# Fifteen small loads into the second K buffer, issued by ScalarE early in a decode block

## Chip, core and metric

The kernel runs on one core of one Trainium2 chip. A core has TensorE (PE), VectorE (DVE), ScalarE (ACT), GpSimd (POOL) and SyncE (SP), and 16 DMA engines that move data between the chip's memory (HBM) and the core's buffers. The metric is device time in microseconds (us); lower is better. The kernel before took 1309.94 us (median of 3 runs, 1309.94 to 1310.12).

## What is computed

One token for each of two sequences: a layer norm of x, a cached attention of 32 query heads over 8 key/value heads with 32768 cached positions, and a gated feed-forward branch that scales the attention's result. All data is float32.

```python
B, Sq, D = 2, 1, 512
Hq, Hkv, Sk, Dh = 32, 8, 32768, 128
...
q = (x @ wq).reshape(B, Sq, Hq, Dh).transpose(0, 2, 1, 3)
k = repeat(k_cache, Hq // Hkv, axis=1); v = repeat(v_cache, Hq // Hkv, axis=1)
p = softmax(einsum("bhqd,bhkd->bhqk", q, k) * Dh ** -0.5)
s = einsum("bhqk,bhkd->bhqd", p, v).transpose(0, 2, 1, 3).reshape(B, Sq, Hq * Dh) @ wo
...
gate = xn @ W_gate
h = gate * (gate > 0) * (xn @ W_up)
g = silu(h @ W_down)
...
xn = layernorm(x)
out = x + s * g
```

The two caches are 268 MB each; everything else is 28 MB. Every cached number is used once.

## The kernel before

The cache is read in 32 pieces of K and 32 of V (`PAIRS`), each of 8.39 MB: 128 partitions with one contiguous run of 64 KB each (`rows_of`, L413). Two K buffers, `kbuf[0]` and `kbuf[1]`, take the K pieces in turn (`load_kk`, L409); one more buffer of the same size, `wide`, takes first the query weights `wq`, then the gate and up weights together (`load_gu`, L544), then the down weights (`load_d`, L602), then one V piece after another (`load_vv`, L428). The output weights `wo` go into `kbuf[1]` at the end.

For each piece of K, VectorE transposes it in place (L660, eight instructions), TensorE forms the scores, and two steps later TensorE multiplies the weights with the V piece of the same positions. After every two pieces a softmax over one head group is finished.

All instructions are written out in one program order by a small class, `Program`. Each operation names the tiles it reads and writes; `op` (L39) derives the semaphore waits. An engine executes its own operations strictly in that order, so a wait also holds up what follows on the same engine. Every DMA goes through `load` (L239): it is issued by SyncE unless `engine="ACT"` is given, and it counts 16 on the semaphore named as its third argument when it has landed.

Before the main loop the order is as follows. SyncE issues `wq` into `wide` (L261) and the first K piece (`load_kk(0)`, L877), which wait for nothing. ScalarE issues two loads of x, of 2 rows of 2 KB (`xp`, in `st0`) and of 8 rows of 512 B (`xy`), at L289 and L290. VectorE computes the layer norm's statistics from `xp`; ScalarE takes the square root (L373 to L377); VectorE's reciprocal (L378) and normalization follow, and TensorE transposes the result. `project_q` (L456) multiplies it by `wq`. When that has freed `wide`, SyncE issues gate and up (`load_gu`) and, right behind them, the second K piece (`load_kk(1)`, L880), whose buffer is empty and which waits for nothing of its own. Inside the loop SyncE then issues the down weights and the third K piece at step 0, and from then on a V piece and a K piece at every step, each when its buffer has been read.

The rows named DMA queue in the profile are q1, which carries SyncE's loads, q10, which carries ScalarE's, and q8 and q14, which carry the engines' instruction code.

Of the kernel before, what the change touches and what calls it, by code (L numbers as in the profile page):

```python
# [162 lines left out]
def decode_block_kernel(nc, x, kc, vc, wq, wo, wg, wu, wd, out):  # L163
# [17 lines left out]
    def sbuf(name, *shape, align=32):  # L181
        return nc.alloc_sbuf_tensor(name, list(shape), F32, align_bytes=align)[:]
# [4 lines left out]
    kbuf = [sbuf(f"k{i}", P, 2 * NC * NR * DH, align=ALIGN) for i in range(2)]  # L187
# [42 lines left out]
    def dve(fn, r=(), w=()):  # L230
        pg.op("DVE", fn, r, w)
# [7 lines left out]
    def load(dst, src, sem, r=(), w=(), engine="SP"):  # L239
        pg.op(engine, lambda e: e.dma_start(dst, src), r, w, dma=sem)  # L240
# [12 lines left out]
    def group(g):  # L253
        return g % B, g // B
# [42 lines left out]
    for kb in range(4):  # L297
        dve(
            lambda e, kb=kb: e.memset(block_of[Q * kb : Q * kb + Q, kb * REP : (kb + 1) * REP], 1.0),
            w=["block_of"],  # L300
# [27 lines left out]
    n = 1  # L328
    while n < Q:
# [45 lines left out]
        ["stat", "eps"],  # L375
        ["stat"],
    )  # L377
    dve(lambda e: e.reciprocal(stat[:, 4:5], stat[:, 3:4]), ["stat"], ["stat"])  # L378
    dve(
        lambda e: e.tensor_scalar(xc, xc, stat[:, 4:5], None, op0=ALU.mult),  # L380
# [10 lines left out]
                lambda e, k=k: e.transpose(  # L391
                    px[:, k * 32 : (k + 1) * 32], xquad[:, k, :], ident[:32, :32]
                )
# [12 lines left out]
    def k_keys(b):  # L406
        return [f"k{b}"] + [f"k{b}_{i}_{c}" for i in range(2) for c in range(NC)]

    def load_kk(j):  # L409
        b = j % 2  # L410
        load(kbuf[b], rows_of(kc, 2 * j), f"k{b}", w=k_keys(b))

    def rows_of(src, t):  # L413
        b, hk = group(t // NU)
        lo = (t % NU) // 2 * 2 * TK
        return src[b, hk, lo : lo + 2 * TK, :].rearrange("(p r) d -> p (r d)", p=P)
# [431 lines left out]
    def project_far():  # L848
# [26 lines left out]
        )  # L875

    load_kk(0)  # L877
    project_q()
    load_gu()
    load_kk(1)  # L880

    for j in range(PAIRS + 2):
# [47 lines left out]
        if j + 2 < PAIRS:  # L930
            load_kk(j + 2)
# [64 lines left out]
```

## Time and profile before

| | |
|---|---|
| time, median of 3 | 1309.94 us |
| span of the profiled execution | 1308.4 us |
| time and span apart | 1.5 us |
| PE busy | 859.0 us (66%) |
| DVE busy | 718.1 us (55%) |
| ACT busy | 51.4 us (4%) |
| DMA, mean over the span | 432 GB/s |
| loads of K, issue to landing | 48.2 us (median of 32) |
| loads of V, issue to landing | 29.6 us (median of 31) |

The profile shows one execution. Its span runs from the first to the last recorded instruction of the core; the time measured from outside is 1.5 us longer. A DMA "packet" in it is one contiguous piece that one of the 16 DMA engines moves, or the count that an engine posts on a semaphore when its part of a load is done (these are the packets under 512 B). A load that is issued while others are still under way queues behind them, so the time from issue to landing is mostly queueing where it is much longer than the bytes need.

### The profile page before, as it was taken

To read this page: it belongs to the slowest core of one execution; us is meant where nothing else is said; L and a number is where in the kernel's file an instruction comes from. 1 tells how busy PE (TensorE), PEld (TensorE's weight loads), DVE (VectorE), ACT (ScalarE), POOL (GpSimd) and SP (SyncE) were. 2 spreads that over 40 slices of the span, in tenths; PEclk is the share of its full clock that TensorE was granted. 3 is DMA by queue.
4 is the path that set the end of the run, shared out by engine and by line. 5 is a ranking of instruction groups with operands and counts; after the bars stand their busy time and mean duration, and the time that the engine had idled before them with its cause. 6 is when DMAs were issued, how large, how long until landed. Compare 5 with 4: busy or idle time off the path is not lost.

```text
span 1308.4 us, 11146 instructions
## 1 busy us (share of the span) xinstructions
PE 859.0 (66%) x4720; PEld 211.5 (16%) x4720; DVE 718.1 (55%) x690; ACT 51.4 (4%) x133; POOL 10.5 (1%) x38
## 2 busy tenths in 40 slices
PE   3566675785666587576667667667665757865676
PEld 1111111211111121111111112121111112111121
DVE  3566654565655456664546666455665545656521
ACT  0001000000000000000000000000000000000000
POOL 0000000000000000000000000000000000000000
PEclk9677788878878887878898778798887889788788
DMA  9999999999999999999999999999999999999998
GB/s 417 423 438 435 437 431 441 425 439 429 437 429 439 435 433 441 429 441 427 439 429 437 429 439 435 433 441 429 441 427 439 429 437 429 439 435 433 439 431 357
DMA packets 10693, 564.79 MB, mean 432 GB/s; under 512 B 1195, under 2 KB 1211, under 8 KB 1597
## 3 DMA queue, kind: packets, MB, share of 16 engines
q1 hardware_dynamic: 10668, 564.67, 99.7%
q8 instruction: 6, 0.10, 0.0%
q14 instruction: 3, 0.02, 0.0%
q10 hardware_dynamic: 16, 0.01, 0.0%
HBM read 564.67 MB, written 0.00 MB: 432 GB/s over the span
## 4 chain that ended last, share of the span: by engine, by line
DMA 64%; DVE 17%; PE 15%; issue 4%; SPq 0%
DMA k<-in_A_k_cache_dram 58%; DVE k L660 17%; PE o L243 8%; PE s L243 6%; DMA k<-in_A_wo_dram 3%; DMA w<-in_A_wq_dram 2%; PE m_ps L243 1%; PE m_ps L693 0%; PE d L243 0%; SPq L240 0%; DVE gy L870 0%; DVE gy L872 0%
## 5 line engine op out<-in xcount | busy, mean ns | idle before, releaser
L243 PE MATMUL s<-k,qcur 128*32 128x512 f32 x2048 | 504.5, 710 | 370.5 <-DVE k L660 370.3
L660 DVE STREAM_TRANSPOSE k<-k 128x2048 f32<-128x2048 f32 x256 | 565.2, 2275 | 147.0 <-DMA k<-in_A_k_cache_dram 147.0
L243 PE MATMUL o<-w,wt 128*16 128x512 f32 x1984 | 245.5, 596 | 9.0 <-DMA w<-in_A_v_cache_dram 9.0
L243 PEld LDWEIGHTS s<-k,qcur 128*32 128x32 f32 x2048 | 89.5, 123 | 785.0 <-DVE k L660 639.3
L737 DVE STREAM_TRANSPOSE wt<-pt 128x512 f32<-128x512 f32 x64 | 45.9, 717 | 139.4 <-PE pt L243 134.6
L678 DVE TENSOR_SCALAR_CACHE_REDUCE st<-s 128x512 f32<-128x512 f32 x64 | 43.0, 672 | 120.9 <-PE s L243 120.9
L243 PEld LDWEIGHTS o<-w,wt 128*16 128x16 f32 x1984 | 62.4, 98 | 167.5 <-issue 167.5
L722 ACT ACTIVATE st<-st,nb 128x512 f32<-128x512 f32 x64 | 45.4, 710 | 1111.0 <-DVE nb L719 1111.0
L243 PE MATMUL pt<-st,perm 128*128 128x512 f32 x128 | 72.6, 696 | 1.5 <-ACT st L722 1.5
L763 DVE RECIPROCAL rl<-m_ps 128x1 f32<-128x1 f32 x16 | 2.7, 169 | 111.0 <-PE m_ps L243 111.0
L243 PE MATMUL m_ps<-ob,heads 128*128 128x128 f32 x128 | 21.7, 321 | 29.0 <-DVE ob L777 29.0
L243 PEld LDWEIGHTS pt<-st,perm 128*128 128x128 f32 x128 | 25.3, 219 | 34.4 <-issue 30.1
L803 DVE STREAM_TRANSPOSE os<-m_ps 128x512 f32<-128x512 f32 x16 | 11.5, 717 | 23.2 <-PE m_ps L243 23.2
L243 PEld LDWEIGHTS m_ps<-ob,heads 128*128 128x128 f32 x128 | 18.0, 217 | 31.1 <-DVE ob L777 31.1
L243 PE MATMUL m_ps<-w,wt 128*32 128x512 f32 (+1 forms) x128 | 16.2, 640 | 8.1 <-DMA w<-in_A_wq_dram 8.1
L777 DVE SCALAR_TENSOR_TENSOR ob<-o,share,ob 128x128 f32<-128x128 f32 x48 | 16.9, 351 | 1.7
L530 POOL TENSOR_TENSOR qcur<-qall,block_of 128x128 f32<-128x128 f32 x16 | 6.5, 406 | 1008.3 <-PE s L243 974.0
L243 PE MATMUL m_ps<-negone,mrow 1*128 1x1 f32 x32 | 6.0, 256 | 9.3 <-DVE mrow L708 9.3
L722 ACT ACTIVATION_READ_ACCUMULATOR st<-st,nb 128x1 f32 x64 | 11.9, 186 | 0.0
L481 DVE COPY os<-m_ps 128x512 f32<-128x512 f32 x2 | 1.4, 692 | 16.3 <-PE m_ps L243 16.3
L243 PE MATMUL o<-k,wt 128*16 128x512 f32 x64 | 8.4, 687 | 2.8 <-DMA k<-in_A_v_cache_dram 2.8
L391 PE MATMUL m_ps<-ident,st 32*128 32x32 f32 x4 | 0.7, 307 | 14.0 <-DVE st L380 14.0
(80 smaller groups left out, 102.8 us busy)
## 6 DMA issues: line engine op xcount, KB each, us to landing
k<-in_A_wo_dram SPq DMA_DIRECT2D x1, 4096.0 KB, 37.3
w<-in_B_W_gate_dram SPq DMA_DIRECT2D x1, 3584.0 KB, 19.6
w<-in_B_W_up_dram SPq DMA_DIRECT2D x1, 3584.0 KB, 27.6
w<-in_B_W_down_dram SPq DMA_DIRECT2D x1, 3584.0 KB, 15.6
k<-in_A_wo_dram SPq DMA_DIRECT2D x1, 2048.0 KB, 41.7
k<-in_A_wo_dram SPq DMA_DIRECT2D x1, 1024.0 KB, 43.7
k<-in_A_k_cache_dram SPq DMA_DIRECT2D x32, 48.2
k<-in_A_wo_dram SPq DMA_DIRECT2D x1, 512.0 KB, 44.5
```

The source lines that it names most:

```text
L243: return lambda e: e.matmul(out_, lhs, rhs, start=start, stop=stop, skip_group_check=True)
L391: lambda e, k=k: e.transpose(px[:, k * 32 : (k + 1) * 32], xquad[:, k, :], ident[:32, :32])
L481: dve(lambda e, q=qs, h=half: e.tensor_copy(q, pq[h]), [f"m{half}"], [f"os{half}"])
L530: lambda e: e.tensor_tensor(qcur.rearrange("p e (k h) -> p e k h", h=REP), qall[:, b, hk].unsqueeze(2).to_broadcast([P, 4, Q // REP, REP]) ...
L660: dve(lambda e: e.transpose(at_, at_), [f"k{t // 2 % 2}"], [key])
L678: lambda e: e.tensor_scalar(st[u], ps_s[t % 2], SCALE, None, op0=ALU.mult, op1=ALU.max, accum_out=mx[:, u : u + 1],),
L722: lambda e, u=u: e.activation(st[u], st[u], AF.Exp, bias=nb, scale=1.0, accum_out=ls[:, u : u + 1]),
L737: dve(lambda e: e.transpose(wt[t % 2], ps_p[t % 2]), [f"pt{t % 2}"], [f"wt{t % 2}"])
L763: dve(lambda e: e.reciprocal(rl, ps_m[1][:, :1]), ["m1"], ["rl"])
L777: lambda e, part=part, c=c: e.scalar_tensor_tensor(ob, part, share[:, c : c + 1], ob, op0=ALU.mult, op1=ALU.add),
L803: lambda e: e.transpose(ot, ps_m[1].rearrange("p (h q j) -> p j h q", h=REP, j=ROWS)),
```

## The change

Fifteen loads are added on ScalarE, behind the square root of the layer norm. Load n copies n rows of 2 KB (n from 1 to 15) from the beginning of `wq` into the first n partitions of `kbuf[1]`, each load into columns of its own. Nothing reads what they bring. They count on one semaphore, `marks`, and each writes a key `mark1` to `mark15`. The second K piece, `load_kk(1)`, overwrites them, and so it now names these keys and waits for all fifteen.

```diff
+    MARKS = 15
+    for n in range(1, MARKS + 1):
+        load(
+            kbuf[1][:n, (n - 1) * 512 : n * 512],
+            wq[:n, :512],
+            "marks",
+            w=[f"mark{n}"],
+            engine="ACT",
+        )
     dve(lambda e: e.reciprocal(stat[:, 4:5], stat[:, 3:4]), ["stat"], ["stat"])
...
     def load_kk(j):
         b = j % 2
-        load(kbuf[b], rows_of(kc, 2 * j), f"k{b}", w=k_keys(b))
+        marks = [f"mark{n}" for n in range(1, MARKS + 1)] if j == 1 else []
+        load(kbuf[b], rows_of(kc, 2 * j), f"k{b}", w=[*k_keys(b), *marks])
```

On ScalarE, at the start of the program, the order before is this (a row is the line, the operation, the tiles and the shape, and in brackets what it waits for; L374 is the square root, L648 the SiLU of the gate, L722 the exponentials):

```order
L240 DMA st<-in_A_x_dram 2x512 [waits sem_DVE]
L240 DMA xy<-in_A_x_dram 8x1x128 [waits sem_DVE]
L374 ACT_TABLE_LOAD
L374 ACTIVATE stat<-stat,eps_t 32x1 [waits sem_DVE]
L648 ACT_TABLE_LOAD
L648 ACTIVATE gy<-d,zero 128x128 [waits sem_PE]
L722 ACT_TABLE_LOAD
```

The same place in the changed program, from the square root on, up to the eleventh of the new loads (the remaining four, of 12 to 15 rows, follow, and then the table load of the SiLU):

```order
L374 ACTIVATE stat<-stat,eps_t 32x1 [waits sem_DVE]
L240 DMA k<-in_A_wq_dram 1x512
L240 DMA k<-in_A_wq_dram 2x512
L240 DMA k<-in_A_wq_dram 3x512
L240 DMA k<-in_A_wq_dram 4x512
L240 DMA k<-in_A_wq_dram 5x512
L240 DMA k<-in_A_wq_dram 6x512
L240 DMA k<-in_A_wq_dram 7x512
L240 DMA k<-in_A_wq_dram 8x512
L240 DMA k<-in_A_wq_dram 9x512
L240 DMA k<-in_A_wq_dram 10x512
L240 DMA k<-in_A_wq_dram 11x512
```

The fifteen loads stand between the square root and the next table load, and none of them waits for anything but its turn on ScalarE.

On SyncE, the first loads of the program before, with the buffers' numbers:

```order
L240 DMA w<-in_A_wq_dram 128x16384
L240 DMA k0<-in_A_k_cache_dram 128x16384
L240 DMA w<-in_B_W_gate_dram 128x7168 [waits sem_PE]
L240 DMA w<-in_B_W_up_dram 128x7168
L240 DMA k1<-in_A_k_cache_dram 128x16384
L240 DMA w<-in_B_W_down_dram 128x7168 [waits sem_PE]
L240 DMA k0<-in_A_k_cache_dram 128x16384
```

And in the changed program:

```order
L240 DMA w<-in_A_wq_dram 128x16384
L240 DMA k0<-in_A_k_cache_dram 128x16384
L240 DMA w<-in_B_W_gate_dram 128x7168 [waits sem_PE]
L240 DMA w<-in_B_W_up_dram 128x7168
L240 DMA k1<-in_A_k_cache_dram 128x16384 [waits sem_marks]
L240 DMA w<-in_B_W_down_dram 128x7168 [waits sem_PE]
L240 DMA k0<-in_A_k_cache_dram 128x16384
```

The order is the same; the fifth load, the second K piece, has gained a wait for the fifteen small ones.

## The prediction

> **What bounds the kernel now.** I read the page's slices and queue totals first.
>
> ```profile
> DMA  9999999999999999999999999999999999999998
> q1 hardware_dynamic: 10668, 564.67, 99.7%
> q8 instruction: 6, 0.10, 0.0%
> q10 hardware_dynamic: 16, 0.01, 0.0%
> HBM read 564.67 MB, written 0.00 MB: 432 GB/s over the span
> ```
>
> All 40 slices have the DMA engines busy. Queue q1 is SyncE's and carries nearly every byte; q10 is ScalarE's, and its 16 packets are the two loads of x. Then the busy time by stretches (columns: stretch, length, busy time of PE, PEld, DVE, ACT, POOL, granted clock, DMA share, GB/s).
>
> ```profile
> 80.00:500.00 420.00, 283.12 (x1496) 67.06 (x1496) 246.51 (x222) 19.22 (x50) 3.45 (x11) 0.82 1.00 434
> 500.00:1000.00 500.00, 331.28 (x1793) 80.86 (x1792) 281.35 (x254) 17.57 (x48) 3.67 (x12) 0.83 1.00 434
> 1000.00:1250.00 250.00, 167.52 (x896) 38.94 (x899) 146.02 (x129) 8.78 (x24) 1.83 (x6) 0.82 1.00 434
> ```
>
> From 80 to 1250 us the DMA share is 1.00 at 434 GB/s, while the busiest other engine works two thirds of the time. So the transfers bound the kernel, and they never wait: whatever time the 16 DMA engines lose early is added to the end. 434/16 = 27.1 GB/s for one engine, so a 64 KB partition row takes 2.42 us, a 28 KB row of the gate or up weights 1.06 us, and a K or V load of 8.39 MB 19.3 us. Last, the chain of waits and SyncE's issues at the start.
>
> ```profile
> 0.74 21.90 DMA w<-in_A_wq_dram
> 32.03 0.33 SPq L240
> 32.40 0.44 SPq L240
> 32.88 46.64 DMA k<-in_A_k_cache_dram
> 79.54 8.90 DVE k L660 x4
> 72.39 0.33 SPq L240 DMA_DIRECT2D w<-in_B_W_down_dram  x1
> w<-in_B_W_up_dram SPq DMA_DIRECT2D x1, 3584.0 KB, 27.6
> ```
>
> At 32.03, 32.40 and 32.88 SyncE issues gate, up and the second K load, k1. They queue behind the first K load. Up lands at 32.40 + 27.6 = 60.0; k1 lands at 79.5, one load's 19.3 us (and 0.2) later. Although k1 is issued at 32.88, its first bytes are not wanted before about 58. This is its **slack: 25 us**. The next issue behind it comes at 72.39.
>
> **The change, part by part.** (1) Bytes: 120 rows of 2 KB are 0.25 MB, 0.57 us at 434 GB/s if spread evenly. (2) ScalarE: fifteen issues after its Sqrt.
>
> ```profile
> 1.42 1.19 ACTq L240 DMA_DIRECT2D st<-in_A_x_dram  x1
> 2.66 0.60 ACTq L240 DMA_DIRECT2D xy<-in_A_x_dram  x1
> 10.13 0.68 DVE L364 TENSOR_REDUCE stat<-st 32x1 f32<-32x512 f32 x1 [2.91 <-DMA st<-in_A_x_dram]
> 12.95 0.29 ACT L374 ACTIVATE stat<-stat,eps_t 32x1 f32<-32x1 f32 x1 [8.38 <-DVE stat L372]
> 102.78 0.37 ACT L648 ACTIVATE gy<-d,zero 128x128 f32<-128x128 f32 x1 [88.23 <-PE d L243]
> ```
>
> At 0.60 to 1.19 us each they fill 13.2 to 22 or 31 us. ScalarE has nothing else until 102.78, so this costs nothing; VectorE's reciprocal waits for the Sqrt, which stays ahead of them. (3) One wait: SyncE issues k1 only when all fifteen have landed. Behind it on SyncE stand the down weights and the third K load; they are not due before 72.39.
>
> So everything hangs on **when the last of the fifteen lands**. The loads of x show how q10 gets its share beside a full q1. I cut the first 18 us into windows: 7.2 to 7.3, 7.3 to 9.7, 9.7 to 9.8, 12.12 to 12.22, 14.55 to 14.65 and 17.0 to 17.1 us. One row of q10 from each, with the q1 row of the second:
>
> ```profile
> q10 hardware_dynamic: 2, 0.00, 10.5%
> q1 hardware_dynamic: 16, 1.05, 100.8%
> q10 hardware_dynamic: 2, 0.00, 0.1%
> q10 hardware_dynamic: 2, 0.00, 1.1%
> q10 hardware_dynamic: 2, 0.00, 3.4%
> q10 hardware_dynamic: 2, 0.00, 3.4%
> q10 hardware_dynamic: 2, 0.00, 1.1%
> ```
>
> The shares tell the packets apart: 10.5% of 16 engines in 0.1 us is 84 ns for each of two packets, x's 2 KB rows (two rows, two engines); 1.1% is 9 ns, the semaphore counts behind them; 3.4% is 27 ns, the 512 B rows of the second load; then its counts. So two engines passed five items of q10 at about 7.25, 9.75, 12.17, 14.6 and 17.05, 2.45 us apart: **one item, data or count, after each 64 KB packet of q1**. Between 7.3 and 9.7 q1 started 16 packets, one an engine. The 2 KB load took from 1.42 to 10.13 this way.
>
> The second load of x began on the same two engines as the first. With one row an engine, counted from the same first engine, a load of n rows uses engines 1 to n, and the first engine has a row and a count of all fifteen: 30 items, hence **30 turns**. They begin behind the last item at 17.05. What q1 still has on that engine then, up to the end of the up weights: two packets and a count of wq, and eight packets and a count each of k0, gate and up: 3 + 9 + 9 + 9 = 30. The window from 17.1 to 59.7 us bears this out, and two more show when up ends (57.9 to 58.7 and 58.7 to 59.7):
>
> ```profile
> q1 hardware_dynamic: 490, 18.48, 100.5%
> q8 instruction: 1, 0.02, 0.1%
> DMA packets 31, 1.01 MB, mean 1265 GB/s; under 512 B 15, under 2 KB 15, under 8 KB 15
> DMA packets 2, 0.07 MB, mean 66 GB/s; under 512 B 1, under 2 KB 1, under 8 KB 1
> ```
>
> 490 less the 16 first packets of k1 is 474, 29.6 an engine. Fifteen engines post up's count at 58.3 on average (middle of the window), one up to 1.3 later. So on the first engine the last of the thirty turns falls just behind the last item of the up weights: the 25 us of slack are used up to the last turn. That engine's own items add 15 x 84 + 14 x 9 ns = 1.4 us: 59.7. From counts to the waiting engine pass 0.35 us (9.75 to 10.13 above). **SyncE issues k1 at 60.0 instead of 32.88**, into a queue that has run dry at 58.3 on most engines.
>
> What a load costs that finds the queue empty, the first one shows (all its counts fall into 21.6 to 22.3 us; the second row is the stretch from 0.74 to 1.70):
>
> ```profile
> DMA packets 32, 1.05 MB, mean 1498 GB/s; under 512 B 16, under 2 KB 16, under 8 KB 16
> 0.74:1.70 0.96, 0.00 (x0) 0.00 (x0) 0.80 (x4) 0.00 (x0) 0.49 (x2) 1.00 0.00 0
> ```
>
> Issued at 0.74, its counts come at 21.95 on average: 21.2 us for 19.3 us of work, so 1.9 us are lost, and 1.0 at the very least, since nothing moves before 1.70. Sum: 60.0 + 1.9 - 58.3 = **3.6 us** for the average engine, 2.7 with the least restart. The bytes are in it, as the engines process them before the gap. One part comes back: the single engine that was late with up (I put it down to the window's one q8 packet, instruction code) waits less, and if it is among those that end last, the end moves by only 2.3. The other five of the page's six q8 packets lie outside the window and keep their effect. I take **3.3 us**, nearer to the average engine.
>
> The Trainium skill, "DMA: Bandwidth & Descriptors", section "Queues, rings and completion order", has each engine go round between rows of rings and drain a whole packet, typically 9 to 17 descriptors, before it switches. By that, thirty items would need some four turns, the loads would land long before 58, and the sum would be the bytes alone, about 1309.94 + 0.57 = 1310.5. The rows above speak against it: two items never shared a turn. The same page, section "Why a DMA increments its semaphore by 16 and not by 1", puts a load of k rows on the lowest-numbered k engines when issued this way; the trace agrees, both loads of x beginning on one pair.
>
> The sum is made on the span of 1308.4 us; the median is 1309.94, 1.5 more. 1308.4 + 3.3 + 1.5 = **1313.2 us**, 0.25% slower. A measurement here tells about 0.2%, 2.6 us, from no change: above 1312.6 is slower.
>
> **The rivals.** (a) *Not slower: the fifteen land in time*, because several of q10's items pass in one turn when many are queued, or because the loads are spread over the engines (120 rows on 16 engines are 8 at most, 16 turns, done by about 43 us). It decides if the count ends three turns earlier than I have it, 3 x 1.06 us, so that k1 is issued about 2 us before 58.3. Then only bytes remain: 0.57 us even, 1.4 us if the first engine has its 15 rows and ends last: 1310.5 to 1311.3. For it: thirty against thirty is a narrow margin, and x shows only five turns, all between 64 KB packets. Against it: all five were single. (b) *The first engine is the late one*, held up by code: the last count comes up to 1.3 later, 1314.5. One of two engines in the x pair could be it. (c) One or two turns fewer: each takes off 1.06 us, 1311.1 to 1312.5. More turns than 30 cost little, since a dry q1 lets the rest pass at 9 to 84 ns. (d) ScalarE's issues stall, or a lone count takes long: over 1315.2. (e) Faster: only if the restart evens out engines that ended late, at most the 1.3 us of one of them, against 2.7 of gap.
>
> **How the numbers follow.** Forecast (1312.6 to 1314.1) 0.57, (a) 0.17, (b) 0.15, (c) 0.07, (d) 0.03, (e) 0.01. The range from 1310.5, the bytes alone, to 1315.2, case (b) with the dearer restart, takes in (a), (b) and (c). Slower by over 0.2%: forecast, (b) and (d), less a little of the forecast's lower edge: 0.73. Same: (a), (c) and that edge: 0.25. Faster 0.02.
>
> **What would show it.** In the profile after: k1's issue at about 60 us, not 32.9, waiting for the DMA of the small loads; a DMA share below 1.00 between 58 and 62 us, with some 3 us of nothing; k1 landing near 82 to 83; then the same 434 GB/s to the end, and q10 with 16 packets plus 120 rows and 120 counts. Wrong if k1 is issued well before 57, if q10's small packets come several to a turn, or if the gap is there and the end does not move by it.

## The result and the profile after

The changed kernel takes 1316.97 us (median of 3, 1316.77 to 1317.32) against 1309.94: a ratio of 1.0053, with a 95% interval of 1.0034 to 1.0073. It is 7.0 us slower, where 3.3 were forecast and 1315.2 was the end of the range. The span of the profiled execution grew from 1308.4 to 1315.2, by 6.8 us.

SyncE's issues and ScalarE's, and the chain of waits at the start, in the changed kernel (start, length, what):

```profile
13.02 5.37 ACTq L240 DMA_DIRECT2D k<-in_A_wq_dram  x15
33.39 0.33 SPq L240 DMA_DIRECT2D w<-in_B_W_gate_dram  x1
33.76 0.43 SPq L240 DMA_DIRECT2D w<-in_B_W_up_dram  x1
63.17 0.33 SPq L240 DMA_DIRECT2D k<-in_A_k_cache_dram  x1
72.22 0.33 SPq L240 DMA_DIRECT2D w<-in_B_W_down_dram  x1
17.98 45.17 DMA k<-in_A_wq_dram
63.17 23.43 DMA k<-in_A_k_cache_dram
86.62 8.89 DVE k L670 x4
```

ScalarE issues the fifteen loads within 5.4 us. The last of them, issued at 17.98, takes 45 us to land, and the second K piece, k1, is issued at 63.17 where it had been 32.88. It lands at 86.6 where it had been 79.5. What the DMA engines did in the stretch from 57 to 67 us shows in 40 slices of 0.25 us (first the busy tenths, then GB/s):

```profile
DMA  7999799550505020020000000000997600000000
GB/s 344 467 459 467 344 573 459 229 229 0 238 0 238 0 115 0 0 115 0 0 0 8 0 0 0 0 0 0 2097 1573 262 262 0 0 0 0 0 0 0 0
```

A packet is counted where it starts. From 58.75 us on fewer and fewer start, as one engine after the other runs out of work, and between 62.5 and 64.0 nothing at all starts. This is the gap. After it the transfers are as before:

```profile
80.00:500.00 420.00, 276.16 (x1492) 65.35 (x1492) 240.83 (x219) 19.22 (x50) 3.46 (x11) 0.82 1.00 433
500.00:1000.00 500.00, 336.70 (x1794) 81.62 (x1794) 283.60 (x254) 17.57 (x48) 3.68 (x12) 0.83 1.00 434
1000.00:1250.00 250.00, 161.70 (x867) 37.75 (x867) 146.82 (x127) 8.79 (x24) 1.84 (x6) 0.83 1.00 435
```

The DMA share is 1.00 throughout, so nothing is caught up later. Which item came last? The queue rows of the page, then the window from 62.3 to 62.5 us:

```profile
q10 hardware_dynamic: 256, 0.25, 0.1%
...
DMA packets 3, 0.00 MB, mean 10 GB/s; under 512 B 2, under 2 KB 2, under 8 KB 3
q10 hardware_dynamic: 2, 0.00, 2.9%
q1 hardware_dynamic: 1, 0.00, 0.3%
```

q10 carried 240 packets more than before, 120 rows and 120 counts. In the window lie one 2 KB row of q10, one count of q1 and one count of q10: the fifteenth row, the count of the up weights, and the fifteenth count. So thirty items did meet thirty, to the last one. Only the time at which this happened was wrong: 62.4 us where 59.7 had been worked out.

### The profile page after: what moved, and what is told of

Same layout as the page of the kernel before. It is cut to its first block, busy times and chain, and to the rows that moved or that the text cites. A ratio compares the mean times of both kernels' runs of the same rounds, so it can differ in the third digit from the quotient of the medians.

```text
span 1315.2 us, 11161 instructions
## 1 busy us (share of the span) xinstructions
PE 854.4 (65%) x4720; PEld 210.5 (16%) x4720; DVE 718.0 (55%) x690; ACT 51.4 (4%) x133; POOL 10.5 (1%) x38
## 4 chain that ended last, share of the span: by engine, by line
DMA 64%; DVE 18%; PE 13%; issue 4%; ACTq 0%; SPq 0%; ACT 0%
DMA k<-in_A_k_cache_dram 56%; DVE k L670 18%; PE o L243 8%; PE s L243 5%; DMA k<-in_A_wo_dram 4%; DMA k<-in_A_wq_dram 3%; DMA st<-in_A_x_dram 1%; ACTq L240 0%; PE m_ps L703 0%; PE m_ps L243 0%; SPq L240 0%; DVE st L371 0%; DVE stat L364 0%; DVE stat L372 0%; DVE st L367 0%
## 5 line engine op out<-in xcount | busy, mean ns | idle before, releaser
L243 PE MATMUL s<-k,qcur 128*32 128x512 f32 x2048 | 497.6, 692 | 380.2 <-DVE k L670 380.0
L243 PEld LDWEIGHTS o<-w,wt 128*16 128x16 f32 x1984 | 62.5, 97 | 165.7 <-issue 165.7
```

Of the source, the lines that this page charges most:

```text
L243: return lambda e: e.matmul(out_, lhs, rhs, start=start, stop=stop, skip_group_check=True)
```

## The experiments

Two questions were open: whether the turns and the gap are the cause at all, and what made the last turn 2.7 us late. My theory for the second was that rows written into partitions 0 to 14 hold up the engines that write these partitions for the large loads. Each kernel is the changed kernel with the edit shown. The time is the median of 3 to 10 runs, and the last column sets it against the kernel before on the same chip (1309.9 to 1310.1 us). The issue of k1 is that of SyncE's row in the one execution that was profiled. Most of these took within 0.4 us of the median, but e2's took 1.8 us more, e8's 0.8 less and e9's 0.7 more.

| kernel | k1 issued, us | time, us | above before |
|---|---|---|---|
| the change | 63.17 | 1316.97 | 7.0 |
| e1 ten loads | 53.07 | 1310.74 | 0.7 |
| e2 one load of 120 rows | 38.76 | 1311.22 | 1.2 |
| e3 fifteen loads of 1 row | 60.09 | 1313.86 | 3.8 |
| e4 partitions 64 to 78 | 61.67 | 1315.85 | 5.8 |
| e5 another tile, 120 partitions | 61.64 | 1315.24 | 5.2 |
| e6 the same without the wait | 33.19 | 1312.15 | 2.1 |
| e7 another source | 63.28 | 1317.20 | 7.2 |
| e8 issued by SyncE | 46.36 | 1313.37 | 3.4 |
| e9 8 rows, four partitions apart | 62.11 | 1315.28 | 5.3 |
| e10 8 rows, partitions 0 to 7 | 63.46 | 1317.14 | 7.1 |
| e11 twelve loads of 1 row | 54.49 | 1310.07 | 0.0 |
| e12 twenty loads of 1 row | 61.75 | 1315.11 | 5.1 |

### Turns and the gap

**e11, e3 and e12: one row a load, twelve, fifteen and twenty loads**

```diff
-    MARKS = 15
+    MARKS = 12        # e3: 15, e12: 20
...
-            kbuf[1][:n, (n - 1) * 512 : n * 512],
-            wq[:n, :512],
+            kbuf[1][:1, (n - 1) * 512 : n * 512],
+            wq[:1, :512],
```

> As e3_one_row_each with twelve loads in place of fifteen: 24 items, so the last count falls behind the third packet of the up weights, six turns earlier. Theory of turns: issue near 54 us (53.5 to 55), before the bytes are wanted, and no cost at all: 1309.8 to 1310.6. Rival, that the small loads cost each its part: 12/15 of the 3.8 us of e3_one_row_each, 1313.1.

> Fifteen loads of one row each, all into partition 0: still 30 items on the first engine, an eighth of the bytes. Theory of turns: the last count again falls behind the up weights, so the gap stays. With the second theory (what made the last count 2.7 us later than forecast is that engines 2 to 15 write into partitions that the first engine's own 64 KB rows share a port with) nothing of that is left here: the second K piece is issued at 60 to 60.8 us and the time is 3.6 to 4.5 us above before, 1313.6 to 1314.4. Rival to the second theory, that the turns themselves are slower than counted: issue at 63 us and 1316.5 to 1317. Rival to the turns: 1310 to 1311.

> As e3_one_row_each with twenty loads: 40 items, ten more than q1 has on that engine before it runs dry. Theory of turns: with q1 empty the last ten pass at 84 and 9 ns each, 0.5 to 1 us in all, so the issue is at 60.5 to 61.5 us and the time 0.4 to 1.4 us above e3_one_row_each, 1314.2 to 1315.3. Rival, that an item takes a microsecond or more whether q1 has work or not: ten more items, issue at 70 us and 1323 or more.

The ratio of e11 is 1.0000 (0.9990 to 1.0010), of e3 1.0029 (1.0018 to 1.0041), of e12 1.0036 (1.0021 to 1.0051). Twelve loads cost nothing and fifteen cost 3.8 us. The chain of waits of e11 shows why (start, length, what). Behind it stands SyncE's issue of k1 in e3:

```profile
16.41 38.06 DMA k<-in_A_wq_dram
54.47 0.02 issue
54.49 25.13 DMA k<-in_A_k_cache_dram
79.62 0.02 issue
79.64 15.47 DVE k L670 x7
```

```profile
60.09 0.33 SPq L240 DMA_DIRECT2D k<-in_A_k_cache_dram  x1
```

The last of the twelve lands at 54.5, six turns earlier than with fifteen; k1 still queues behind the up weights and lands at 79.6, where it landed before. In e3 the thirty turns can be read off one by one. The trace records the start and the duration of every packet, and on a busy engine each starts within some nanoseconds of the end of the one before, so the packets of the first engine can be followed back from the last count, at 59.61, to the first small row, at 19.59 us. One of q10 and one of q1 take turns all the way. With twenty loads ten items are left over when q1 is dry. The window from 60.3 to 60.9 us of e12:

```profile
DMA packets 12, 0.01 MB, mean 17 GB/s; under 512 B 7, under 2 KB 7, under 8 KB 12
q10 hardware_dynamic: 11, 0.01, 4.9%
q1 hardware_dynamic: 1, 0.00, 0.1%
```

Eleven items of q10 pass in 0.6 us, and only one of q1, a count, among them. A turn is long only because of what q1 moves between. The issue came 1.7 us after e3's, where 1.4 at most were expected.

**e1: ten loads of 1 to 10 rows** (`MARKS = 10`)

> The change with ten small loads in place of fifteen (1 to 10 rows). Theory of turns (one item of q10 passes the first DMA engine after each item of q1): 20 items, so the last passes at the end of the gate weights, near 53 us; the second K piece is issued at 53 to 55 us, before its bytes are wanted (about 58 us less the 1.9 us that an issue into an empty queue costs), and there is no gap. What is left is the lateness that the small loads give to single engines: 0.5 to 2 us, 1310.5 to 1312. Rival, that the small loads cost by their bytes or their number: 55 of 120 rows, 10 of 15 loads, so 3.2 to 4.7 us of the 7.0, 1313 to 1315.

Ratio 1.0005 (0.9996 to 1.0015), k1 issued at 53.07. Two thirds of the loads and 55 of the 120 rows stay, and a tenth of the cost. A cost by bytes or by number of loads would have been 3 us and more.

**e2: one load of 120 rows**

```diff
-    MARKS = 15
-    for n in range(1, MARKS + 1):
...
+    MARKS = 1
+    load(kbuf[1][:120, :512], wq[:120, :512], "marks", w=["mark1"], engine="ACT")
```

> One load of 120 rows of 2 KB in place of fifteen: the same bytes and the same wait, 8 rows and one count on each of 15 engines. Theory of turns: 9 items, the last near 40 us, so the second K piece is issued at its old place behind the up weights, 33 to 42 us, and nothing is lost but the bytes: 0.5 to 1.2 us, 1310.5 to 1311.2. Rival, that the bytes or the wait as such cost the time: about 1317 as with the change.

Ratio 1.0009 (0.9999 to 1.0018). The same bytes with the same wait, but nine items on an engine: landed and k1 issued at 38.76.

**e5 and e6: the rows in another tile, with the wait and without it.** The 120 rows go to 120 partitions of a score tile that is written next near 100 us; its writer then waits for them. e6 also takes them out of what k1 waits for:

```diff
-        load(
-            kbuf[1][:n, (n - 1) * 512 : n * 512],
...
+        lo = n * (n - 1) // 2
+        load(st[2][lo : lo + n, :], wq[:n, :512], "marks", w=[f"mark{n}"], engine="ACT")
...
-        marks = [f"mark{n}" for n in range(1, MARKS + 1)] if j == 1 else []
-        load(kbuf[b], rows_of(kc, 2 * j), f"k{b}", w=[*k_keys(b), *marks])
+        load(kbuf[b], rows_of(kc, 2 * j), f"k{b}", w=k_keys(b))
```

> The change with the 120 rows written to 120 different partitions of a score tile that is idle then (st2), so that they spread over all partitions; the second K piece still waits for them. Theory of shared ports: the first engine's partitions get about a seventh of the foreign rows that they get with the change, so the last count comes 2 to 2.7 us earlier: issue at 60.2 to 61.2 us, 3.9 to 5 us above before, 1313.9 to 1315.1. Rival, that many small loads in flight slow all engines wherever they write: issue at 61.7 to 63.2 us, 1315.8 to 1317.2.

> As e5_other_tile_wait, with the wait of the second K piece taken away (the score tile's first writer, near 100 us, waits instead). Theory of the gap: the issue is back at 33 us, there is no gap, and what is left is bytes and the lateness of single engines: 0.5 to 2 us, 1310.5 to 1312. Rival, that the small loads cost by disturbing the big ones: within 1 us of e5_other_tile_wait, 1313 to 1316.

Ratios 1.0040 (1.0026 to 1.0054) and 1.0016 (1.0007 to 1.0026). The same loads cost 5.2 us with the wait and 2.1 without it, so the wait is worth 3.1 us here. The 2.1 us are just above the 2 that were allowed for the bytes and the lateness of single engines; no run separates the two. e5's issue, 61.64, and its time lie between what the theory of ports and its rival gave.

**e8: the loads issued by SyncE**, behind the first K piece and so in q1

```diff
-            engine="ACT",
...
     load_kk(0)
+    for n in range(1, MARKS + 1):
+        load(kbuf[1][:n, (n - 1) * 512 : n * 512], wq[:n, :512], "marks", w=[f"mark{n}"])
     project_q()
```

> The same fifteen loads with the same wait, issued by SyncE between the first K piece and the gate weights, so that they stand in q1 and take no turns. Theory of turns: they pass right behind the first K piece, near 42 to 45 us; the second K piece is issued at 43 to 46 us, there is no gap, 0.5 to 2 us above before, 1310.5 to 1312. Rival, that bytes, number or wait cost the time: 1316 to 1317.5.

Ratio 1.0026 (1.0016 to 1.0036). In q1 they take no turns, and k1 is issued at 46.36, 0.4 later than expected and with no gap. But the cost was 3.4 us, more than the 2 allowed. The stretch from 42 to 46 us, where they pass, in e8 and then before:

```profile
42.00:46.00 4.00, 0.01 (x1) 0.01 (x1) 2.38 (x2) 0.00 (x0) 0.00 (x0) 0.50 1.01 279
```

```profile
42.00:46.00 4.00, 0.33 (x1) 0.18 (x2) 2.69 (x2) 0.00 (x0) 0.00 (x0) 0.50 1.07 459
```

There e8 moves 180 GB/s less for 4 us, 0.7 MB or 1.7 us of full rate. From 36 to 42 us it moves 379 GB/s against 424, another 0.6 us, and from 46 to 52 it gains 0.1. That is 2.2 of the 2.5 us by which the span of this execution was longer than before (1310.9 against 1308.4). In its trace the 120 rows take 0.20 us each on average, against 84 ns in e3. So packed closely in q1 they cost much more than their bytes; why is open.

### What made the last turn late

e3 holds the first answer: with thirty items on the first engine and none on the others, k1 is issued at 60.09, which is what the prediction had for the change (60.0). So the engine's own items, the turns and the way to SyncE were right, and what is missing comes from the other fourteen engines' items. How the large packets fare shows in the window from 24 to 28 us, where 32 packets of 64 KB start in each kernel: the change, and then e3 (the last column is the time that the packets took, as a share of 16 engines).

```profile
q1 hardware_dynamic: 32, 2.10, 126.8%
q10 hardware_dynamic: 28, 0.03, 2.3%
```

```profile
q1 hardware_dynamic: 32, 2.10, 120.9%
q10 hardware_dynamic: 2, 0.00, 0.1%
```

1.268 x 16 x 4 / 32 is 2.54 us for a packet with the change, and 2.42 with e3, which is also what it was before. While 28 items of q10 pass, the large packets are stretched by 5%.

For the first engine this can be added up. Between its first small row, at 19.6 us in both kernels, and its last count, at 59.61 in e3 and 62.44 with the change, it moves 25 large packets. Followed back in the trace as above, it is never idle for more than some nanoseconds between items; with e3 the large packets take 0.05 us more in all than 2.418 us for each 64 KB and 1.062 us for each 28 KB, and with the change about 2.7 us more (2.5 to 2.8, as a few packets end too close together to tell the engines apart). So the lateness of the last turn is the sum of what the first engine's own large packets took longer.

**e4: the rows in partitions 64 to 78**

```diff
-            kbuf[1][:n, (n - 1) * 512 : n * 512],
+            kbuf[1][64 : 64 + n, (n - 1) * 512 : n * 512],
```

> The change with the rows written to partitions 64 to 78 in place of 0 to 14. Theory of shared ports: partitions 64 and up belong to the second half of the engines, so the first engine is no longer held up by other engines' rows; the last count comes 2 to 2.7 us earlier, the second K piece is issued at 60.3 to 61.3 us, and the time is 3.9 to 5 us above before, 1313.8 to 1315. Rival, that reading the same few rows of the query weights, or the number of loads in flight, slows the engines: issue at 63 us and 1316.5 to 1317.3 as with the change.

Ratio 1.0045 (1.0029 to 1.0062). k1 is issued at 61.67, 1.5 us earlier than with the change and 0.4 later than the theory allowed: between the two. e5 above, with its rows over all partitions, gives the same 61.64. In both the first engine's 25 large packets take about 1.3 us longer, half of what they do with the change.

**e7: another source**

```diff
-            wq[:n, :512],
+            wo[:n, :512],
```

> The change with the rows read from the output weights (2 KB rows that follow one another) in place of the query weights (2 KB rows 16 KB apart). If reading is what slows the large packets while the small loads are under way, the issue moves by a microsecond or more, to 61 to 62 us and 1314.8 to 1316; if writing or turns are, it stays at 63 us and 1316.7 to 1317.3.

Ratio 1.0054 (1.0037 to 1.0071), issue 63.28: no difference from the change. These two layouts of the rows in HBM cost the same.

**e9 and e10: fifteen loads of 8 rows**, written four partitions apart, or close together

```diff
-            kbuf[1][:n, (n - 1) * 512 : n * 512],
-            wq[:n, :512],
+            kbuf[1][0:32:4, (n - 1) * 512 : n * 512],      # e10: kbuf[1][:8, ...]
+            wq[:8, :512],
```

> Fifteen loads of 8 rows each (120 rows, 30 items on each of the first eight engines), the rows written four partitions apart (0, 4, ... 28). If what slows the large packets is that several engines write into partitions whose 64 KB rows another engine moves, each of the eight now keeps to its own, nothing is slowed, and the second K piece is issued at 59.8 to 60.8 us: 1313.5 to 1314.5. Rival, that many small loads in flight slow all engines wherever they write: issue at 61.5 to 63 us, 1315 to 1317.

> As e9_eight_spread, with the rows written to partitions 0 to 7, which belong to two engines. Theory of shared ports: each of these two engines' partitions gets 45 foreign rows of 84 ns, 3.8 us, so its last count comes that much later: issue at 63 to 64.5 us, 1316.5 to 1318. Rival: as e9_eight_spread within 0.5 us.

Ratios 1.0040 (1.0025 to 1.0055) and 1.0057 (1.0039 to 1.0075). Bytes, loads, engines and turns are the same in both; only the partitions differ, and 1.9 us with them. The packets that start from 58 to 60.2, from 60.2 to 62.2 and from 62.2 to 63 us, in e9 and then in e10 (those under 512 B are counts, of the up weights and of the small loads). The last line is q1's part of e10's last window:

```profile
DMA packets 40, 0.48 MB, mean 216 GB/s; under 512 B 16, under 2 KB 16, under 8 KB 24
DMA packets 24, 0.04 MB, mean 22 GB/s; under 512 B 16, under 2 KB 16, under 8 KB 23
DMA packets 0, 0.00 MB, mean 0 GB/s; under 512 B 0, under 2 KB 0, under 8 KB 0
```

```profile
DMA packets 42, 0.33 MB, mean 151 GB/s; under 512 B 23, under 2 KB 23, under 8 KB 31
DMA packets 9, 0.12 MB, mean 58 GB/s; under 512 B 4, under 2 KB 4, under 8 KB 5
DMA packets 6, 0.00 MB, mean 5 GB/s; under 512 B 4, under 2 KB 4, under 8 KB 6
...
q1 hardware_dynamic: 2, 0.00, 0.1%
```

In e9 seven of the eight engines post their last count between 60.5 and 61.0 us and the eighth at 61.76. In e10 six are through by 60.3, and two, whose counts of the up weights are the two packets of q1 in the last window, end at 62.5 and 62.85: two engines are held up, and they set the wait. These two end 2.9 and 3.2 us later than the first engine in e3, the other six 0.4 to 0.6. That agrees with the Trainium skill, "SBUF — State Buffer", section "Door 1: The DMA port swizzle (why `[64,N]` ≈ `[32,N]`)", by which four neighbouring partitions share one of 16 ports, so that partitions 0 to 7 are two of them and 0 to 14 four. But k1 was issued at 62.11 in e9 and not at 60.8 at most, and its time, 1315.28, is what the rival gave, so sharing of ports is not all of it.

## Why the prediction was right and wrong

- *The transfers bound the kernel and never wait, so a gap is added to the end*: right. The sum with the measured issue in place of the forecast one, 63.17 + 1.9 - 58.3, is 6.8 us, and the span grew by 6.8.
- *Thirty turns, one item after each item of q1, on the first engine*: right. The last row, up's count and the last count stand side by side at 62.4 us; twelve one-row loads cost nothing and fifteen 3.8 us; without the wait 3.1 of 5.2 us go.
- *A load into an empty queue loses 1.9 us*: right for most engines. The counts of k1 in the changed kernel, in the windows from 84.1 to 84.6 and from 84.6 to 86.2 us:

```profile
DMA packets 28, 0.40 MB, mean 803 GB/s; under 512 B 14, under 2 KB 14, under 8 KB 14
DMA packets 18, 0.46 MB, mean 287 GB/s; under 512 B 2, under 2 KB 2, under 8 KB 2
```

  Fourteen of sixteen come about 84.35, 21.2 us after the issue, the figure taken from the first load. The other two come up to 1.8 us later. With them and the later issue k1 landed at 86.6, where 82 to 83 were forecast.
- *ScalarE's issues cost nothing*: right; its next work, the SiLU, waits for the down weights as before.
- **The step that failed** is the term "That engine's own items add 15 x 84 + 14 x 9 ns = 1.4 us: 59.7", and with it "SyncE issues k1 at 60.0". The mechanism stood; the term was too small. It priced the items of the first engine alone and left the other engines' 105 rows at nothing for it. With them that engine's large packets took about 2.7 us longer in all, and the last count came at 62.4, 2.7 us later. Without them (e3) the issue is at 60.09 and the time at 1313.86, within 0.7 us of the forecast.
- *0.35 us from the counts to SyncE*: in the changed kernel 0.7, from 62.45 to 63.17. A smaller miss on the same side.
- *0.3 us given back at the end by an engine that was late anyway*: did not show; 6.8 of gap and 6.8 of span leave no room for it.
- The range ended at 1315.2 because it allowed the first engine to be 1.3 us late, by instruction code, and not 2.7, by large packets that take longer.

Of the 3.1 us between the issues of the change and of e3, about 1.5 go when the rows are moved away from partitions 0 to 14 (e4, e5). In the change the rows pile up on these few partitions, which few engines' large loads write, and e10 against e9 shows the same pile with all else equal. The other 1.5 stay when many engines carry small loads, wherever these write (e4, e5) and, as far as tried, from wherever they read (e7). What they are is open. In e9 a part of the lateness has another cause, in that execution at least. A packet of q8, instruction code, runs from 41.95 to 42.83 us, and the counts that one of the eight engines posts behind the first K piece come at 42.82, 0.7 us after those of the other seven. The engine that ends last ends 0.8 us after the others, and by the order of its items it is the same one. But those seven too end 0.9 to 1.4 us later than the first engine in e3, though each engine's rows are four partitions from the next one's.

## What to carry to other kernels

A small load beside a full queue is not paid in bytes but in turns: on every engine that it uses, each of its rows and its count waits for one packet of the other queue, 2.4 us where these are 64 KB. A wait for it is free until the last turn reaches the time when the waiting load's bytes are wanted, and from there each microsecond counts in full, with the restart of the empty queue on top; so count the turns on the busiest engine, and let one load with many partitions take the place of many small ones (1.2 us against 7.0 here). When you count, price the other engines' items too.

## What was not expected of the hardware

- Small rows stretch other engines' large packets: 2.54 us in place of 2.42 for 64 KB while 28 small items passed in 4 us. In the same window it is 2.43 in e5, with as many items and other partitions, and 2.42 in e3, with two items.
- Where 120 small rows are written matters by 1.9 us (e9, e10), with the same loads, engines and bytes.
- In one queue with the large loads the same fifteen loads still cost 3.4 us (e8), though the wait for them opened no gap.
